# Attention, mixing and a channel network on one core: conversions spread later, other planner durations, 24 passes

## The chip, the cores and the metric

The kernel runs on one core of a Trainium2 chip. The time is what the device takes for one execution, in microseconds (us); a kernel's time is the median of its runs. TensorE does the matmuls and is called PE in the profile, with its weight loads apart (PEld); VectorE is DVE, ScalarE is ACT, GpSimd is POOL, and SyncE (SP) issues the transfers between DRAM and the core's memory.

## The reference

Three stages, one behind the other, in float32. The attention has windows: half of the heads see the last 32 positions, the others every fourth of the last 128.

```
B, H, S, D = 4, 8, 576, 64                 # q, k, v
a = softmax(mask(q @ k^T / 8)) @ v          # windowed; heads put side by side: x is (4, 576, 512)
xk = mu_k*x + (1-mu_k)*x_prev;  xr = mu_r*x + (1-mu_r)*x_prev      # x_prev: one position earlier
x = sigmoid(xr @ w_r) * (relu(xk @ w_k)**2 @ w_v)                   # 512 -> 1024 -> 512
u = x + (x^T @ U @ V)^T                                             # U 576x32, V 32x576
out = u + relu(u @ w_ch1) @ w_ch2                                   # 512 -> 2048 -> 512
```

## The kernel before

**Phase one** is the attention and the mixing step. The mixing step works on eight chunks of 288 positions. Chunk 0 multiplies whole float32 weights (L811). From chunk 1 on each operand is split into a high and a low part, and a product is three matmuls, L814 (high by high), L815 (low weight), L816 (low input). The splits of the twenty weight pieces are `hi_lo` by way of `sub`, and the subtraction is L348 on VectorE (`wl<-wx,wh`). A chunk is 20 steps, called quanta: four `r` tiles (they need weight pieces 1 to 4), eight `k` tiles (pieces 5 to 12), and the `v` tiles (13 to 20), 24 matmuls for two such steps of eight products. Inside each chunk two *visits* bring the attention forward, two units at a time out of 32: scores `qk` (L675, `psS<-raw`), masks and row maxima on VectorE (L536), exponentials on ACT, the inverse of the row sums on VectorE (L550, L551), normalisation on POOL (L556), transposes on PE (`tr`, L713), a copy of them on ACT (`pts`), and the product with v (`pv`, L731). So the matmuls of attention come in packs of up to 160 small ones between the large ones of the mixing step.

**The weights** come as 64-bit words and are converted on the chip by `cv_bits`: one operation on ACT (L384) and four on VectorE (L385, L386, L388, L391). `jobs` is the list of these: 20 for the mixing weights, then 32 for the channel network (`cv_w2`, whose result goes back to DRAM as `w2f`, L418), one for U and two for V. `convert_to(n)` brings the list forward to job n; in chunk c from 1 on it is called in every quantum with 20 + 0.35 times the number of quanta since chunk 1 began.

**Phase two** starts while phase one ends: y is read back, the U step and the V step follow (L907, L925, L926, L943; L948 adds to `us`), u goes through DRAM (`uf`) and comes back as `ug`. The channel network multiplies in combined blocks: the sums of weight blocks (L471) feed `ch1` (L1035 to L1037), split rows (`rh`, `rl`, L348) feed `ch2` (L1112 to L1114).

**The order of the work** isn't that of the code. Each operation is only recorded, with its engine, a duration that the code estimates, what it reads and writes, and sometimes `lock=True` (VectorE and POOL are planned not to run two such operations at once). `plan()` then goes through the list forwards, taking what can start first by those durations, computes backwards how late each could be, and repeats with that as the rank, `PASSES` times in all; the order with the earliest planned end is written out, for every engine. Where the plan sees PE wait for more than 900 ns ahead of an operation that opens a bank, it puts filler matmuls by a tile of zeros there (L1304), for half of that time. Their number so depends on the planned durations, and nothing else that is issued on PE changes in number with the plan.

Of the kernel before, what the change touches and what calls it, by code (L numbers as in the profile page):

```python
# [18 lines left out]
NCH = 2 * B  # L19
# [37 lines left out]
VISIT0 = (4, 12)  # L57
VISIT = (1, 10)
CONV0 = [min(20, 7 + n) for n in range(20)]
W2RATE = 0.35  # L60
SIDE_AT = 9
SPLIT = (-4, -4, -3, -3, -1, -1, 0, 0, 1, 1, 2, 2, 5, 5, 6, 6, 7, 7, 8, 8)
SPLIT_ENG = ("DVE",)
# [6 lines left out]
LATE = 1500.0  # L70
FILL, FILL_FROM, FILL_NS = 0.5, 900.0, 0.453
PLAN_PRINT = None
PASSES = 10
RATE = 285.0


# [1 line left out]
def tile_attention_mix_channel(  # L78
# [44 lines left out]
    def op(eng, ns, fn, r=(), w=(), more=100, lock=False, mode=None, size=0):  # L123

        o = Op()
        o.eng, o.ns, o.fn, o.r, o.w, o.more, o.lock, o.mode, o.size = eng, ns, fn, list(r), list(w), more, lock, mode, size
        ops.append(o)
# [214 lines left out]
    def sub(eng, n, out_, a, b, r, w, psum=False, fr=True):  # L342

        if eng == "POOL":
            t = 50 + 2.45 * n if fr else 110 + 1.93 * n
            op("POOL", t, lambda: nc.gpsimd.tensor_tensor(out=out_(), in0=a(), in1=b(), op=ALU.subtract), r, w, 40, lock=True)  # L346
        else:
            dve(n, lambda: nc.vector.tensor_tensor(out=out_(), in0=a(), in1=b(), op=ALU.subtract), r, w, two=True, psum=psum)  # L348
# [228 lines left out]
    def attend(u):  # L577

        b, part, pair = unit(u)
        nw, kc, starts, mk = unit_kind(pair, part)
        raw = raws.pop(u)
        sc = [bank("S") for _ in range(2)]
        pr = Lazy([P, 10 * KW], F32, "pr", "pr", 4)
        mn, sm = Lazy([P, 5], F32, "mn", "mn", 3), Lazy([P, 5], F32, "sm", "sm", 3)
        pt, ov = bank("S"), bank("S")
        pts = Lazy([P, 5 * P], F32, "pt", "pts", 2)

        def qk():  # L590
            for w in range(nw):
                for e in range(2):
                    r = head(e)
                    k0 = nw * QW + starts[w]
                    slot, h = (w // 4, w % 4) if w < 8 else (2, 2 * e + w - 8)
                    nc.tensor.matmul(
                        sc[e]()[h * QW : (h + 1) * QW, slot * KW : (slot + 1) * KW],
                        lhsT=raw()[r, w * QW : (w + 1) * QW], rhs=raw()[r, k0 : k0 + KW], start=True, stop=True,
                    )

        pe(nw * 2 * 40, qk, [(raw, 0)], [(x,) for x in sc], "qk")
        yield
        slots = [(e, s_ * KW, (2 * s_ + e) * KW, mk[s_]) for s_ in range(2) for e in range(2)]

        def lows():
            for i, (e, c, d, m) in enumerate(slots):
                low(sc[e](), c, pr(), d, m, mn(), i)
            for e in range(2):
                low(sc[e](), 2 * KW, pr(), 4 * KW, mk[2], mn(), 4, head(e))

        def exps():
            for i in range(5):
                exp(pr(), i * KW, mn(), sm(), i)

        def norms():
            norm(pr(), 4 * KW, sm(), 4, 1, 5 * KW)
            norm(pr(), 0, sm(), 0, 5)

        op("DVE", 6 * LOW, lows, [(x,) for x in sc] + [("cst",)], [(pr,), (mn,)], 170)
        op("ACT", 5 * EXP, exps, [(pr,), (mn,)], [(pr,), (sm,)], 190, mode="exp")  # L620
        op("DVE", 260, lambda: inv(sm(), 5), [(sm,)], [(sm,)], 80)
        op("POOL", 360 + 6 * NORM, norms, [(pr,), (sm,)], [(pr,)], 40, lock=True)
        yield

        def tr():
            for i in range(3):
                nc.tensor.transpose(pt()[:, i * P : (i + 1) * P], pr()[:, i * P : (i + 1) * P], ident)

        pe(3 * 108, tr, [(pr,), ("cst",)], [(pt,)], "tr")
        yield  # L630
        copy(3 * P, lambda: pts()[:, : 3 * P], lambda: pt()[:, : 3 * P], [(pt,)], [(pts, 0)], psum=True)
        yield

        def pv():
            for w in range(nw):
                for e in range(2):
                    r = head(e)
                    c = (w // 4 * 4 + w % 4 if w < 8 else 8 + 2 * e + w - 8) * QW
                    nc.tensor.matmul(
                        ov()[r, w * QW : (w + 1) * QW], lhsT=raw()[r, QKW + w * D : QKW + (w + 1) * D],  # L640
                        rhs=pts()[r, c : c + QW], start=True, stop=True,
                    )

        pe(nw * 2 * 60, pv, [(pts, 0), (raw, "v")], [(ov,)], "pv")
        yield
        x_out(ov, pair, part, b)
        yield

    def attend2(ua, ub):
# [10 lines left out]
        sm = [Lazy([P, 5], F32, "sm", "sm", 3) for _ in range(2)]  # L660
        pt, ov = bank("S"), [bank("S") for _ in range(2)]
        pts = Lazy([P, 5 * P], F32, "pt", "pts", 2)
        ns = nw // 2
# [19 lines left out]
        for e in range(2):  # L683
            first_, own = (ns - 4, 0) if e else (0, 4)
            base = e * ns * KW

            def lows(e=e, first_=first_, own=own, base=base):
                for i in range(4):
                    low(sc[e](), i * KW, pr(), base + (first_ + i) * KW, mk[i // 2], mn[e](), first_ + i)
                if nw == 10:  # L690
                    for f in range(2):
                        low(sc[f](), (4 + e) * KW, pr(), base + own * KW, mk[2], mn[e](), own, head(f))

            def exps(e=e, base=base):
                for i in range(ns):
                    exp(pr(), base + i * KW, mn[e](), sm[e](), i)

            kp, ks = [(pr, e)], [(sm[e],)]
            op("DVE", (4 + 2 * (ns - 4)) * LOW, lows, [(x,) for x in (sc if nw == 10 else sc[e : e + 1])] + [("cst",)], kp + [(mn[e],)], 170)
            op("ACT", ns * EXP, exps, kp + [(mn[e],)], kp + ks, 190, mode="exp")  # L700
            op("DVE", 260, lambda e=e: inv(sm[e](), ns), ks, ks, 80)
            op("POOL", 180 + ns * NORM, lambda e=e, base=base: norm(pr(), base, sm[e](), 0, ns), kp + ks, kp, 40, lock=True)
        yield

# [435 lines left out]
    NQ = 20  # L1140
# [6 lines left out]
    NW = len(places)  # L1147
    jobs = []
    for i, j in places:
        jobs.append((w1raw[i][:, j * CW : (j + 1) * CW], CW, lambda raw, i=i, j=j: cv_weight(raw, (i, j))))  # L1150
    jobs += [
        (w2raw[i][:, j * CW : (j + 1) * CW], CW, lambda raw, i=i, j=j: cv_w2(raw, i, j)) for i in range(16) for j in range(2)
    ]
    jobs.append((upk, NT * RANK, cv_u))
    jobs += [(vpk[:, j * HS : (j + 1) * HS], HS, lambda raw, j=j: cv_v(raw, j)) for j in range(2)]
    loaded = []
    converted = 0
    AHEAD = 3
# [69 lines left out]
    for c in range(NCH - 1):  # L1228
        cur = quanta(c) if c else first
        for n in range(NQ):  # L1230
# [13 lines left out]
            for when, p, which in MIX:  # L1244
                if when == n + 1:
                    mix(c + 1, p, which)
    convert_to(len(jobs))


    prep = {}  # L1250
    for j in range(3):
# [2 lines left out]
        prep[at_ + 1] = lambda j=j: load_rows(2 * j, "DVE")  # L1254
        prep[at_ + 2] = lambda j=j: load_rows(2 * j + 1, "DVE")
    for i, fn in enumerate(quanta(NCH - 1)):
        fn()
        if side:
            side.pop(0)()
        if i in prep:  # L1260
            prep[i]()
    for fn in side:
        fn()

# [134 lines left out]
```

## Time and profile before

| | |
|---|---|
| median of 3 runs | 766.39 us (764.46 to 767.51) |
| the profiled execution | 765.77 us, span 763.9 us, mean granted clock 0.995 |
| PE busy | 739.0 us, 97% of the span, 6925 matmuls |
| VectorE busy | 570.7 us, 75%, 1335 instructions |
| ACT, POOL busy | 391.4 us (51%), 388.3 us (51%) |
| DMA | 109.77 MB, mean 144 GB/s |

The profile is one execution. Busy time is by engine; "idle before" is how long an engine did nothing ahead of a row, and the name behind the arrow is what ended that by the semaphores. "issue" there means that the profile has nothing to name. The granted clock is PE's, as a part of full speed. In the timeline, neighbouring rows of one kind are merged, with their number behind x.

### The profile page before, as it was taken

How to read it: one execution, taken by the hardware profiler on the slowest of the kernel's cores; microseconds unless marked ns; L12 is line 12 of the kernel's file. 1: busy time of each engine (PE TensorE's matmuls, PEld its weight loads, DVE VectorE, ACT ScalarE, POOL GpSimd, SP SyncE). 2: the span in 40 equal slices, each digit the busy share in tenths (PEclk: the TensorE clock that was granted, in tenths of full speed). 3: DMA queues.
4: the chain of work that ended last, by engine and by line, in shares of the span. 5: the costliest groups of instructions: out<-in, count | busy, mean ns of one | idle time of the engine just before them, and what ended most of it. 6: DMA issues, size and time to landing. Idle time of an engine off the chain costs nothing. (4 is left out here: it accounts for less than half of the span.)

```text
span 763.9 us, 18346 instructions
## 1 busy us (share of the span) xinstructions
PE 739.0 (97%) x6925; PEld 678.4 (89%) x6925; DVE 570.7 (75%) x1335; ACT 391.4 (51%) x995; POOL 388.3 (51%) x408
## 2 busy tenths in 40 slices
PE   7898999999999999999899999999999999999997
PEld 5776899899988999999899888888988999898986
DVE  6998999999998644465767789766888865575632
ACT  5686885757684755273444543443452433343310
POOL 1343345646463735274755677534677654456500
PEclk9999999999999999999999999999999999999999
DMA  9874648686867320355553244132432212042001
GB/s 334 275 259 164 204 156 282 210 270 210 281 209 218 117 87 2 124 174 187 178 162 123 71 157 146 56 110 88 162 103 98 84 56 84 28 139 65 19 1 55
DMA packets 53224, 109.77 MB, mean 144 GB/s; under 512 B 5649, under 2 KB 15889, under 8 KB 53137
## 3 DMA queue, kind: packets, MB, share of 16 engines
q1 hardware_dynamic: 53136, 108.62, 43.1%
q8 instruction: 54, 0.88, 0.5%
q14 instruction: 34, 0.27, 0.1%
HBM read 86.05 MB, written 22.54 MB: 142 GB/s over the span
## 5 line engine op out<-in xcount | busy, mean ns | idle before, releaser
L346 POOL TENSOR_TENSOR cl<-sums,ch 128x512 fp32r<-128x512 f32 x72 | 98.2, 1364 | 86.8 <-ACT ch L351 58.5
L1113 PE MATMUL psS<-hh,rl 128*128 128x512 f32 (+1 forms) x320 | 119.6, 374 | 2.6 <-DVE rl L348 2.6
L1114 PE MATMUL psS<-hl,rh 128*128 128x512 f32 (+1 forms) x320 | 119.8, 374 | 0.3 <-DVE hl L1050 0.2
L1112 PE MATMUL psS<-hh,rh 128*128 128x512 f32 (+1 forms) x320 | 119.6, 374 | 0.2 <-ACT hh L1091 0.2
L351 ACT ACTIVATE ch<-sums 128x512 fp32r<-128x512 f32 (+1 forms) x104 | 57.3, 561 | 105.6 <-DVE sums L471 99.9
L814 PE MATMUL psM<-xk,wh 128*128 128x288 f32 x336 | 100.7, 300 | 0.9 <-DVE y L876 0.9
L816 PE MATMUL psM<-xk,wh 128*128 128x288 f32 x336 | 98.9, 294 | 1.5 <-issue 1.5
L815 PE MATMUL psM<-xk,wl 128*128 128x288 f32 x336 | 99.1, 295 | 1.1 <-issue 1.1
L346 POOL TENSOR_TENSOR cl<-st,ch 128x256 fp32r<-128x256 f32 x80 | 66.6, 849 | 56.0 <-PE psM L1037 35.7
L471 DVE TENSOR_TENSOR sums<-st 128x256 f32<-128x256 f32 (+1 forms) x144 | 86.6, 650 | 9.2 <-POOL cl L346 5.6
L346 POOL TENSOR_TENSOR xk<-m,xk 128x288 fp32r<-128x288 f32 x56 | 53.0, 959 | 55.5 <-ACT xk L351 33.3
L1113 PEld LDWEIGHTS psS<-hh,rl 128*128 128x128 f32 x320 | 60.7, 190 | 12.2 <-DVE rl L348 2.8
L1114 PEld LDWEIGHTS psS<-hl,rh 128*128 128x128 f32 x320 | 60.7, 190 | 12.2 <-DVE hl L1092 1.0
L1112 PEld LDWEIGHTS psS<-hh,rh 128*128 128x128 f32 x320 | 60.6, 189 | 10.2 <-ACT hh L1091 0.6
L814 PE MATMUL psM<-k2s,wh 128*128 128x288 f32 x224 | 68.1, 304 | 0.3 <-DVE k L861 0.2
L815 PE MATMUL psM<-k2s,wl 128*128 128x288 f32 x224 | 66.8, 298 | 0.7 <-issue 0.7
L816 PE MATMUL psM<-k2s,wh 128*128 128x288 f32 x224 | 66.7, 298 | 0.0
L814 PEld LDWEIGHTS psM<-xk,wh 128*128 128x128 f32 x336 | 63.0, 187 | 3.1 <-issue 1.6
L816 PEld LDWEIGHTS psM<-xk,wh 128*128 128x128 f32 x336 | 63.2, 188 | 1.2 <-issue 1.2
L815 PEld LDWEIGHTS psM<-xk,wl 128*128 128x128 f32 x336 | 63.1, 188 | 0.1
L1072 DVE TENSOR_TENSOR ok<-ok,psM 128x256 f32<-128x256 f32 (+1 forms) x96 | 46.4, 504 | 20.8 <-PE psM L1037 18.6
L346 POOL TENSOR_TENSOR k2s<-k,k2s 128x288 fp32r<-128x288 f32 x49 | 45.2, 926 | 31.7 <-ACT k2s L351 29.4
(152 smaller groups left out, 2124.0 us busy)
## 6 DMA issues: line engine op xcount, KB each, us to landing
st<-w2f SPq DMA_DIRECT2D x96, 256.0 KB, 3.0
w<-w2raw SPq DMA_DIRECT2D x32, 512.0 KB, 4.8
w<-w1raw SPq DMA_DIRECT2D x20, 512.0 KB, 5.6
w2f<-w SPq DMA_DIRECT2D x32, 256.0 KB, 2.7
raw<-qk SPq DMA_DIRECT2D x16, 320.0 KB, 6.4
ytmp<-y SPq DMA_DIRECT2D x32, 144.0 KB, 3.1
yb<-ytmp SPq DMA_DIRECT2D x4, 1152.0 KB, 6.2
uf<-us SPq DMA_DIRECT2D x32, 144.0 KB, 1.9
```

Source lines behind the costliest of these rows:

```text
L346: op("POOL", t, lambda: nc.gpsimd.tensor_tensor(out=out_(), in0=a(), in1=b(), op=ALU.subtract), r, w, 40, lock=True)
L351: act(n, lambda: nc.scalar.activation(out_(), in_(), AF.Copy), r, w, psum, strided)
L471: dve(k * Q, lambda: nc.vector.tensor_tensor(out=q(sm_, n, k)(), in0=a(), in1=b(), op=op_), [(s1,), (s2,)], [(sm_, key)], two=True)
L814: nc.tensor.matmul(a, lhsT=wh, rhs=xh, start=start, stop=False)
L815: nc.tensor.matmul(a, lhsT=wl, rhs=xh, start=False, stop=False)
L816: nc.tensor.matmul(a, lhsT=wh, rhs=xl, start=False, stop=stop)
L1072: dve(k * Q, lambda: nc.vector.tensor_tensor(out=out_(), in0=a(), in1=b(), op=op_), r, w, two=True, psum=True)
L1112: nc.tensor.matmul(a, lhsT=wh, rhs=xh, start=(j == 0 and e == 0), stop=False)
L1113: nc.tensor.matmul(a, lhsT=wl, rhs=xh, start=False, stop=False)
L1114: nc.tensor.matmul(a, lhsT=wh, rhs=xl, start=False, stop=(j == 7 and e == 1))
```

## The change

The rate of the conversions is 0.28 a quantum for 0.35, and `convert_to` goes on through the last chunk; the jobs for U and V stand behind the first 25 of the 32 jobs of phase two. The planner takes 165 + 2.14 n ns for a subtraction of n columns on POOL, counts the inverse of the sums as `lock`, and runs 24 passes.

```diff
-W2RATE = 0.35
+W2RATE = 0.28
+UV_AT = 25
...
-PASSES = 10
+PASSES = 24
...
         if eng == "POOL":
-            t = 50 + 2.45 * n if fr else 110 + 1.93 * n
+            t = 165 + 2.14 * n if fr else 110 + 1.93 * n
...
-        op("DVE", 260, lambda: inv(sm(), 5), [(sm,)], [(sm,)], 80)
+        op("DVE", 260, lambda: inv(sm(), 5), [(sm,)], [(sm,)], 80, lock=True)
...
-            op("DVE", 260, lambda e=e: inv(sm[e](), ns), ks, ks, 80)
+            op("DVE", 260, lambda e=e: inv(sm[e](), ns), ks, ks, 80, lock=True)
...
-    jobs += [
+    w2_jobs = [
         (w2raw[i][:, j * CW : (j + 1) * CW], CW, lambda raw, i=i, j=j: cv_w2(raw, i, j)) for i in range(16) for j in range(2)
     ]
+    jobs += w2_jobs[:UV_AT]
     jobs.append((upk, NT * RANK, cv_u))
     jobs += [(vpk[:, j * HS : (j + 1) * HS], HS, lambda raw, j=j: cv_v(raw, j)) for j in range(2)]
+    jobs += w2_jobs[UV_AT:]
...
-    convert_to(len(jobs))
...
     for i, fn in enumerate(quanta(NCH - 1)):
+        convert_to(NW + int(((NCH - 2) * NQ + i + 1) * W2RATE))
         fn()
         if side:
             side.pop(0)()
         if i in prep:
             prep[i]()
+    convert_to(len(jobs))
```

The lines of the changed kernel are numbered one higher than before, down to the list of jobs. Three places show what the plan makes of it.

PE at the end of chunk 0 and the start of chunk 1, before (L811 is chunk 0's product, L1304 the filler, L814 and L815 the first of chunk 1):

```order
L675 MATMUL psS<-raw 32x64 x40
L811 MATMUL psM<-xk_293,wx 128x288 x16
L1304 MATMUL psM<-zero 128x512 x4
L811 MATMUL psM<-k_774,wx 128x288 x16
L713 MATMUL psS<-cst_t,pr 128x128 x5
L1304 MATMUL psS<-zero 128x512 x2
L731 MATMUL psS<-pts,raw 64x32 x40
L675 MATMUL psS<-raw 32x64 x40
L1304 MATMUL psM<-zero 128x224 x4
L811 MATMUL psM<-k_774,wx 128x288 x16
L713 MATMUL psS<-cst_t,pr 128x128 x5
L814 MATMUL psM<-xk,wh 128x288
L815 MATMUL psM<-xk,wl 128x288
```

The same place in the changed kernel (L812, L815, L816 are the same products there):

```order
L676 MATMUL psS<-raw 32x64 x40
L812 MATMUL psM<-xk_293,wx 128x288 x4
L812 MATMUL psM<-k_762,wx 128x288 x24
L714 MATMUL psS<-cst_t,pr 128x128 x5
L812 MATMUL psM<-k_762,wx 128x288 x4
L732 MATMUL psS<-pts,raw 64x32 x40
L676 MATMUL psS<-raw 32x64 x40
L812 MATMUL psM<-k_762,wx 128x288 x4
L815 MATMUL psM<-xk,wh 128x288
L816 MATMUL psM<-xk,wl 128x288
L817 MATMUL psM<-xk,wh 128x288
L815 MATMUL psM<-xk,wh 128x288
```

The fillers are gone here, the last piece of attention before chunk 1 comes four products earlier, and one pack of transposes no longer stands ahead of chunk 1.

VectorE at that time, before, from the end of a row of masks (L536) to the weight splits (L348, `wl<-wx,wh`):

```order
L536 ISA pr,mn<-psS,cst_t 64x64
L536 ISA mn 64x1
L348 TENSOR_TENSOR wl<-wx,wh 128x512
L876 TENSOR_TENSOR y<-psM,sg 128x288
L768 SCALAR_TENSOR_TENSOR m<-d,mu_t,x_95 128x288
L550 TENSOR_SCALAR sm<-sm 128x5
L551 RECIPROCAL sm<-sm 128x5
L348 TENSOR_TENSOR wl<-wx,wh 128x512
L876 TENSOR_TENSOR y<-psM,sg 128x288
L768 SCALAR_TENSOR_TENSOR m<-d,mu_t,x_964 128x288
L550 TENSOR_SCALAR sm<-sm 128x5
L551 RECIPROCAL sm<-sm 128x5
L348 TENSOR_TENSOR wl<-wx,wh 128x512 x3
```

And in the changed kernel (L349 is the split, L537 the mask):

```order
L769 SCALAR_TENSOR_TENSOR m<-d,mu_t,x_95 128x288
L877 TENSOR_TENSOR y<-psM,sg 128x288
L769 SCALAR_TENSOR_TENSOR m<-d,mu_t,x_95 128x288
L349 TENSOR_TENSOR wl<-wx,wh 128x512
L877 TENSOR_TENSOR y<-psM,sg 128x288
L769 SCALAR_TENSOR_TENSOR m<-d,mu_t,x_95 128x288
L349 TENSOR_TENSOR wl<-wx,wh 128x512 x3
L769 SCALAR_TENSOR_TENSOR m<-d,mu_t,x_95 128x288
L349 TENSOR_TENSOR wl<-wx,wh 128x512
L877 TENSOR_TENSOR y<-psM,sg 128x288
L537 ISA pr,mn<-psS,cst_t 128x64
L537 ISA mn 128x1
```

The masks that stood ahead of the first split now stand behind the fifth, and the two inverse pairs are not among the splits.

VectorE in the last chunk, where phase two begins, before (L471 the first sums, L948 the additions of the U and V step):

```order
L768 SCALAR_TENSOR_TENSOR m<-d,mu_t,x_3263 128x288
L348 TENSOR_TENSOR k2s<-k_1488,k2s 128x288
L768 SCALAR_TENSOR_TENSOR m<-d,mu_t,x_3263 128x288
L348 TENSOR_TENSOR yl<-psS,yh 64x512
L768 SCALAR_TENSOR_TENSOR m<-d,mu_t,x_3263 128x288
L471 TENSOR_TENSOR sums<-st 128x256
L768 SCALAR_TENSOR_TENSOR m<-d,mu_t,x_3263 128x288
L471 TENSOR_TENSOR sums<-st 128x256
L348 TENSOR_TENSOR g<-psS,g 32x512
L876 TENSOR_TENSOR y<-psM,sg 128x288 x2
L948 TENSOR_TENSOR us<-psS,yb 128x288 x2
L876 TENSOR_TENSOR y<-psM,sg 128x288
L948 TENSOR_TENSOR us<-psS,yb 128x288
```

And in the changed kernel, from the like place on (L386, L387, L389 and L392 are a conversion's four operations, L472 the sums, L949 the additions):

```order
L349 TENSOR_TENSOR k2s<-k_1351,k2s 128x288
L769 SCALAR_TENSOR_TENSOR m<-d,mu_t,x_3210 128x288
L349 TENSOR_TENSOR g<-psS,g 32x512
L386 TENSOR_SCALAR w_4805<-w_4805 128x512
L877 TENSOR_TENSOR y<-psM,sg 128x288
L387 TENSOR_SCALAR w_4805<-w_4805 128x512
L472 TENSOR_TENSOR sums<-st 128x256
L389 SCALAR_TENSOR_TENSOR w_4805<-w_4172,w_4805 128x512
L949 TENSOR_TENSOR us<-psS,yb 128x288 x2
L877 TENSOR_TENSOR y<-psM,sg 128x288
L392 SCALAR_TENSOR_TENSOR w_4805<-w_4172,w_4805 128x512
L386 TENSOR_SCALAR w_4828<-w_4828 128x512
```

Between the same sums and additions there are now conversions.

## Rows read from the trace of the kernel before

**Rows 1.** The page, section 1: busy us, share of the span, instructions, by engine

```profile
PE 739.0 (97%) x6925; PEld 678.4 (89%) x6925; DVE 570.7 (75%) x1335; ACT 391.4 (51%) x995; POOL 388.3 (51%) x408
```

**Rows 2.** Busy time by stretch: stretch, length, engines (instructions), granted clock, DMA share, GB/s

```profile
50.00:100.00 50.00, 46.52 (x601) 39.24 (x579) 47.35 (x151) 37.91 (x115) 16.83 (x20) 1.00 0.61 204
...
250.00:300.00 50.00, 50.00 (x674) 48.98 (x673) 25.85 (x86) 30.69 (x90) 25.52 (x35) 1.00 0.21 71
...
300.00:350.00 50.00, 50.00 (x370) 48.90 (x369) 29.07 (x56) 27.35 (x58) 27.04 (x31) 1.00 0.39 126
```

**Rows 3.** Timeline, PE: start, us, line, operation, [idle before <- releaser]

```profile
89.48 0.40 PE L814 MATMUL psM<-xk,wh 128*128 128x288 f32 x1 [0.93 <-DVE y L876]
...
177.21 0.29 PE L815 MATMUL psM<-xk,wl 128*128 128x288 f32 x1 [1.05 <-issue]
...
196.95 0.40 PE L815 MATMUL psM<-k2s,wl 128*128 128x288 f32 x1 [0.72 <-issue]
...
215.58 0.29 PE L816 MATMUL psM<-xk,wh 128*128 128x288 f32 x1 [1.54 <-issue]
215.71 0.29 PE L814 MATMUL psM<-xk,wh 128*128 128x288 f32 x1
...
232.83 0.30 PE L675 MATMUL psS<-raw 64*32 64x64 f32 x4 [1.80 <-issue]
```

**Rows 4.** Busy time between the five waits of rows 3

```profile
89.48:177.21 87.73, 85.77 (x1148) 83.76 (x1149) 84.69 (x234) 58.66 (x172) 46.29 (x52) 1.00 0.69 221
177.21:196.95 19.74, 19.02 (x255) 18.48 (x254) 19.63 (x64) 15.19 (x42) 13.26 (x15) 1.00 0.77 253
196.95:215.58 18.63, 17.09 (x254) 16.69 (x255) 17.47 (x56) 12.45 (x42) 8.20 (x11) 1.00 0.81 264
215.58:232.83 17.25, 15.45 (x256) 15.08 (x256) 16.25 (x29) 13.61 (x37) 11.34 (x13) 1.00 0.67 211
```

**Rows 5.** The page, section 3: the instruction queue's packets, MB, share of 16 DMA engines

```profile
q8 instruction: 54, 0.88, 0.5%
```

**Rows 6.** Timeline, PE: a piece of attention ahead of the wait at 177.21

```profile
173.67 1.37 PE L731 MATMUL psS<-pts,raw 64*64 64x32 f32 x80
174.97 0.86 PE L675 MATMUL psS<-raw 64*32 64x64 f32 x64
175.75 0.40 PE L814 MATMUL psM<-xk,wh 128*128 128x288 f32 x1
```

**Rows 7.** Busy time by stretch: behind the last wait, and a later visit

```profile
232.80:236.00 3.20, 3.17 (x17) 3.08 (x17) 2.08 (x24) 2.79 (x10) 1.15 (x2) 0.61 0.88 231
262.00:272.00 10.00, 10.00 (x191) 9.70 (x190) 5.40 (x24) 8.03 (x18) 7.02 (x11) 1.00 0.04 13
```

**Rows 8.** Timeline, PE: waits before the first products of chunk 1

```profile
69.61 0.55 PE L713 MATMUL psS<-cst_t,pr 128*128 128x128 f32 x3 [1.59 <-POOL pr L556]
...
82.73 0.55 PE L713 MATMUL psS<-cst_t,pr 128*128 128x128 f32 x3 [0.52 <-POOL pr L556]
83.03 0.38 PE L814 MATMUL psM<-xk,wh 128*128 128x288 f32 x1
```

**Rows 9.** Timeline, DVE: two groups of weight splits

```profile
81.44 3.00 DVE L348 TENSOR_TENSOR wl<-wx,wh 128x512 fp32r<-128x512 f32 x3
...
85.97 1.28 DVE L348 TENSOR_TENSOR wl<-wx,wh 128x512 fp32r<-128x512 f32 x2
```

**Rows 10.** Busy time of line 536 alone, 12 masks and 12 reads

```profile
75.60:77.82 2.22, 2.08 (x24) 1.00 0.99 328
```

**Rows 11.** Busy time of the tile w alone (conversions of phase two)

```profile
73.00:235.00 162.00, 80.62 (x118) 20.83 (x31) 0.00 (x0) 1.00 0.71 229
```

**Rows 12.** Timeline, PE: a wait for data inside chunk 2

```profile
147.76 0.55 PE L713 MATMUL psS<-cst_t,pr 128*128 128x128 f32 x3 [0.56 <-POOL pr L556]
```

**Rows 13.** Timeline, DVE and PE: the phase boundary

```profile
367.90 1.30 DVE L1017 TENSOR_TENSOR tmp<-ug 128x512 f32<-128x512 f32 x2 [4.11 <-DMA ug<-uf]
...
379.54 0.39 PE L1113 MATMUL psS<-hh,rl 128*128 128x256 f32 x1 [2.61 <-DVE rl L348]
```

## The prediction

> **What bounds the kernel now.** I read the page's first section before anything else. TensorE's matmuls are busy for 739.0 of the span's 763.9 us [rows 1], so a gain must come out of the 24.9 us in which they are not, or out of matmuls at the lower clock, or out of filler matmuls. Next the busy time by stretch: between 50 and 100 us PE is busy for 46.52 of 50 and VectorE for 47.35; from 250 to 350 PE doesn't idle at all and VectorE is down to 25.85 and 29.07 [rows 2]. The work that the change takes later goes there.
>
> Then I listed PE's waits in order of time. Five of them stand out: 0.93, 1.05, 0.72, 1.54 and 1.80 us, at 89.48, 177.21, 196.95, 215.58 and 232.83 us [rows 3]. Four have no releaser that the profile knows ("issue"); the 0.93 is put down to VectorE. Count the matmuls between them: 1148, 255, 254, 256 [rows 4], that is 9, 2, 2 and 2 times some 128. A wait for data would not keep to such a grid. The page has 54 packets of 0.88 MB on the instruction queue [rows 5], 16 KB each; 6925 matmuls and as many weight loads [rows 1] are 13,850 instructions, and over 54 that is 256 apiece, or 128 matmuls. So I read these waits as PE waiting for its next block of instructions.
>
> Why at these and not at the other 45 edges? Each stands just behind a piece of attention, whose matmuls pass in 16 ns each (80 in 1.30 us, 64 in 0.78 us by their starts), where the mixing products before and after take 0.13 us each [rows 3, 6]. A block of 128 that is nearly all attention is used up in 2.0 us, one of products in 17. By my count along PE's order the blocks before the five waits hold 127, 127, 113, 114 and 128 attention matmuls: 2.0, 2.0, 3.7, 3.6 and 2.0 us long. With the wait behind each, a block took 2.9, 3.1, 4.4, 5.1 and 3.8 us to come, in stretches with a DMA share of 0.67 to 0.81 [rows 4]. A block of the same make at 262 to 272 us, share 0.04 [rows 7], has no wait. So: a wait where a whole visit of attention falls into one block while the DMA engines are busy.
>
> **The change, part by part.** The sum is made against the profiled execution, 765.77 us; it lies 0.6 under the median of 766.39.
>
> *Fillers, and with them the grid.* The planner, with 24 passes and other durations, now finds less room in front of chunk 0's matmuls and writes 22 fewer filler matmuls, all before the first of the five waits, and it shifts what stands around each visit. The ends of the visits against the block edges were 1, 15, 14, 4 and 3 matmuls off the nearest edge; by the same count they are now 23, 49, 36, 30 and 19 off for most of the busy stretch. The blocks there hold 105, 79, 92 and 98 attention matmuls: the rest, 23 to 49 products at 0.13 us, makes them 4.6 to 7.6 us long, against the 2.9 to 5.1 us that a block took to come. Those waits go: before, the five cost 6.0 us together. One later block, near 245 us, keeps 127 attention matmuls, a wait of 0 to 1.8; with the DMA still busy there I take 1.2. Another early block of 3.4 us may wait; I take 0.3.
> The clock goes with it. Behind the 1.80 us wait the granted clock reads 0.61 over 3.2 us [rows 7], so most of that stretch ran at the lower of the two levels, 1.2 GHz for 2.4. The 17 matmuls in it, the last 4 of the attention and 13 products, would take 4 x 0.016 + 13 x 0.133 = 1.8 us at the upper one: 1.4 lost. For a wait of 1.2 us I take 0.5, since only the longest of the five shows such a row. So 7.4 us before, 2.0 after: -5.4. Bounds: -7.4 (none is left) to +1.0 (they only move, and one more appears).
> The Trainium skill speaks against this term: "Runtime: NRT & Kernel Launch", Instruction fetch mechanics, says that the sequencer fetches 16 KiB blocks of 256 instructions ahead of use and that the cost of crossing a boundary is "mostly hidden". By that rule this term would be near 0 and the sum near -1.1. The block size agrees with the 54 packets and the counts of 254 to 256; for "hidden" the waits of 0.72 to 1.80 us at those edges decide, as far as the releaser "issue" can be read so.
>
> *VectorE's order at the first chunk's end.* The first mixing products of chunk 1 need the first four weight splits. In before the fourth stands inside the group at 81.44 us, and products start at 83.03 behind waits of 1.59 and 0.52 us for POOL's normalisation [rows 8, 9]. In the new order 12 mask operations with their 12 reads, two inverse pairs and two L768 no longer stand ahead of the fourth split: such a group of 12 masks and 12 reads holds VectorE for 2.08 us [rows 10]; the rest, at 0.3 a pair and 0.4 an L768 by their starts, for 1.4: 3.5 us. But ahead of the eighth split the counts come out level (the masks are in again), and the k products, which need it, may not start before about 87.3 us, the end of the split group of 85.97 [rows 9]. In before they start some 3.2 us after 89.48, at 92.7; the new order has one piece of attention (2.8 us) less in front of them. So PE can get there at most 92.7 - 2.8 - 87.3 = 2.6 us better, 0.9 of it the wait at 89.48 that is already counted. I take -1.7; bounds -4 (ahead of the sixteenth split VectorE has 26 operations fewer, and all of it may show) to +1 (the lost fillers leave PE waiting in their place).
>
> *Conversions at 0.28 a quantum.* Nothing is added: 32 jobs as before. One job is 80.62 us over 118/4 on VectorE, 2.73 us [rows 11]. Before, jobs end with quantum 100 of 140; now with 125. Seven jobs, 19 us, leave the stretch where VectorE is full and land where it has 20 us of room in each 50 [rows 2]. What it gives PE before 235 us: only the waits for data there, 0.56 us at 147.76 [rows 12] and a few tenths. The replanned chunks may as well have one such piece more as one less; a piece in one of six chunks cost 0.9, I take +0.6, bounds -1 to +1.5.
> U and V go before the last seven w2 jobs, so the U step doesn't wait for the later ones. `lock` for the inverses keeps them out of POOL's way in the plan only; POOL's new cost and 24 passes add no instruction. 0, beyond the order counted above.
>
> *Phase boundary.* u and ug go through DRAM; VectorE waits 4.11 us for ug and PE 2.61 us for VectorE's split behind it [rows 13]. The order there is nearly as before: 0, bounds -1 to +2 here, the dearer case is a rival.
>
> Sum: -5.4 - 1.7 + 0.6 = -6.5, so 759.3 for the execution and, 0.6 above it, 759.9 for the median.
>
> **The rivals.**
> A, the grid is an accident or the blocks wait elsewhere: only the start and the data waits count, 766.4 - 1.1 = 765.3. For it: "issue" names no cause, and 0.93 us has a data releaser; edges move with every matmul, so others can be hit. Against it: four counts in a row on multiples of 128. The rule of the Trainium skill that is quoted above ("Runtime: NRT & Kernel Launch") would end here too.
> B, VectorE holds the start as before (47.35 of 50 busy [rows 2], and level counts at the eighth split): 766.4 - 5.4 + 0.6 = 761.6.
> C, slower: the last conversions delay the phase boundary. In the new order five jobs stand among the first sums (L471) and the additions that make u (L948); the stores of u, ug's load and the w2f reads that the sums need queue on SP behind their loads. If nothing hides them, u comes 5 x 2.73 = 13.7 us later, and PE with it: 759.9 + 13.7 = 773.6. For it: VectorE's wait for ug is already 4.11 us, so the chain is late today. Against it: VectorE idles 24 and 21 us in the two stretches from 250 to 350 [rows 2]. It decides from a delay of about 11 us on, where the gain above is gone and half a per cent more.
> D, the planner's order is no better on the chip than before: 766.4.
>
> **How the numbers follow.** Forecast 0.45; B 0.14; A 0.17; D 0.08; C 0.11; 0.05 for a larger gain (all waits gone, start -4: 754). Half a per cent, 3.8 us, is about what a measurement of this kernel tells from no change: faster is under 762.6, slower above 770.2. Faster: 0.42 of the forecast's 0.45 + 0.09 of B's 0.14 + the 0.05 + 0.03 from A's lower end = 0.59. Slower: C's share above 770.2 with 0.02 from the others: 0.12. Same: 0.29. The range is 754 to 768: below, the larger gain; above, A and D with the upper bounds of the small terms, C left out. The likeliest case alone: 757 to 762.
>
> **What would show it.** Right: at the counts of the old grid, no "issue" waits above 0.5 us between 170 and 240 us, and PE idle 6 us lower; the granted clock 1.00 from 100 to 240 us; the first L814 earlier than 83.0 us, k products from about 87 to 90; VectorE's w tile work reaching to about 340 us. Wrong: "issue" waits of the same sum on another multiple of 128 (A); PE busy at its end but started at 83 (B); a wait for ug over 8 us or PE waiting at 356 to 380 us for sums, rh or us (C).

## The result, and the profile after

The changed kernel takes 757.91 us (median of 6 runs, 757.27 to 761.51) against 767.32 for the kernel before in the same comparison: ratio 0.9896, 95% interval 0.9869 to 0.9922, about 8.0 us by the ratio and 9.4 by the medians. Forecast were 759.9 and a gain of 6.5. The profiled execution has a span of 756.0 us for 763.9. Three executions of 1437 to 1446 us, one each of the kernel before, b_spread and a_noclamp below, do not count in the ratios.

Three stages can be compared by PE's timeline: from the start to the first product of chunk 1, from there to the last product of the mixing step, and the rest.

| | before | after | difference | forecast |
|---|---|---|---|---|
| first product of chunk 1 at | 83.0 | 83.4 | +0.4 | -1.7 |
| from it to the last product | 272.8 | 265.9 | -6.9 | -4.8 |
| from it to the span's end | 408.1 | 406.6 | -1.5 | 0 |

So most of the gain sits in the stretch where the five waits were. Busy time by stretch, the kernel after (columns as in [rows 2]; 350 us is where its mixing step has ended):

```profile
0.00:83.00 83.00, 73.05 (x1036) 55.26 (x1037) 71.27 (x234) 55.51 (x171) 24.12 (x36) 0.96 0.75 257
83.00:350.00 267.00, 265.07 (x3295) 259.79 (x3294) 222.95 (x619) 175.52 (x498) 144.71 (x167) 1.00 0.55 184
100.00:250.00 150.00, 150.00 (x2277) 147.47 (x2271) 140.94 (x424) 106.71 (x324) 85.45 (x99) 1.00 0.64 212
```

The like stretches of the kernel before:

```profile
0.00:83.00 83.00, 72.80 (x1064) 56.15 (x1065) 71.71 (x256) 57.55 (x190) 26.88 (x40) 1.00 0.76 263
83.00:356.00 273.00, 266.06 (x3286) 260.16 (x3285) 217.99 (x594) 173.07 (x480) 140.87 (x163) 0.99 0.55 178
100.00:250.00 150.00, 143.98 (x1955) 140.57 (x1954) 142.25 (x398) 101.09 (x292) 81.27 (x91) 0.99 0.71 229
```

PE idled 6.94 us between chunk 1's start and the end of the mixing step, now 1.93; between 100 and 250 us it idled 6.02, now not at all. Just ahead of that window the kernel after has a wait for data, the longest left in its mixing step:

```profile
99.80 1.37 PE L732 MATMUL psS<-pts,raw 64*64 64x32 f32 x80 [1.05 <-ACT pts L352]
```

The waits of PE, longest first, in the kernel after, answer to [rows 3, 8] (us in total, times, longest): no row names "issue" any more.

```profile
PE psM L828 <- DVE xk L769: 3.0, 2, 2.5
PE psM L812 <- ACT sg L352: 1.6, 1, 1.6
PE psS L640 <- ACT pts L352: 1.6, 2, 1.4
PE psS L1308 <- DVE zero L1304: 1.5, 1, 1.5
PE psS L1113 <- DVE us L949: 1.1, 1, 1.1
PE psS L732 <- ACT pts L352: 1.1, 1, 1.1
```

At the phase boundary, timeline of VectorE and PE, kernel after (answering to [rows 13]): VectorE's wait for ug is longer, PE's is shorter.

```profile
361.65 1.30 DVE L1018 TENSOR_TENSOR tmp<-ug 128x512 f32<-128x512 f32 x2 [4.66 <-DMA ug<-uf]
363.34 1.30 DVE L349 TENSOR_TENSOR rl<-st,rh 128x512 fp32r<-128x512 f32 x1
...
363.37 0.38 PE L1113 MATMUL psS<-hh,rh 128*128 128x256 f32 x1 [1.11 <-DVE us L949]
```

The split `rl` comes right behind ug at 363.34; in the kernel before PE stood 2.61 us for one [rows 13]. And the fillers are fewer, as counted: 6903 matmuls for 6925.

### The profile page after: what moved, and what is told of

The parts are those of the page before. It is cut to its first block, busy times and chain, and to the rows that moved or that the text cites. A ratio compares the mean times of both kernels' runs of the same rounds, so it can differ in the third digit from the quotient of the medians.

```text
span 756.0 us, 18304 instructions
## 1 busy us (share of the span) xinstructions
PE 736.8 (97%) x6903; PEld 675.2 (89%) x6903; DVE 569.9 (75%) x1335; ACT 392.3 (52%) x995; POOL 386.9 (51%) x408
## 5 line engine op out<-in xcount | busy, mean ns | idle before, releaser
L815 PE MATMUL psM<-xk,wh 128*128 128x288 f32 x336 | 101.0, 301 | 0.0
L816 PE MATMUL psM<-xk,wl 128*128 128x288 f32 x336 | 99.1, 295 | 0.0
L472 DVE TENSOR_TENSOR sums<-st 128x256 f32<-128x256 f32 (+1 forms) x144 | 85.9, 644 | 8.0 <-POOL cl L347 3.9
L347 POOL TENSOR_TENSOR xk<-m,xk 128x288 fp32r<-128x288 f32 x56 | 54.6, 990 | 33.9 <-ACT xk L352 24.5
L815 PE MATMUL psM<-k2s,wh 128*128 128x288 f32 x224 | 67.3, 301 | 0.0
L816 PE MATMUL psM<-k2s,wl 128*128 128x288 f32 x224 | 66.0, 295 | 0.0
L817 PE MATMUL psM<-k2s,wh 128*128 128x288 f32 x224 | 65.9, 294 | 0.0
L815 PEld LDWEIGHTS psM<-xk,wh 128*128 128x128 f32 x336 | 63.0, 187 | 0.6
L816 PEld LDWEIGHTS psM<-xk,wl 128*128 128x128 f32 x336 | 63.1, 188 | 0.1
L1093 DVE SCALAR_TENSOR_TENSOR hl<-ort,hh 128x512 fp32r<-128x512 f32 x32 | 26.2, 819 | 48.3 <-ACT hh L1092 48.3
```

The costliest lines, as they stand in the source:

```text
L472: dve(k * Q, lambda: nc.vector.tensor_tensor(out=q(sm_, n, k)(), in0=a(), in1=b(), op=op_), [(s1,), (s2,)], [(sm_, key)], two=True)
L815: nc.tensor.matmul(a, lhsT=wh, rhs=xh, start=start, stop=False)
L816: nc.tensor.matmul(a, lhsT=wl, rhs=xh, start=False, stop=False)
L817: nc.tensor.matmul(a, lhsT=wh, rhs=xl, start=False, stop=stop)
```

## The experiments

Theory G: a block of instructions that is nearly all attention is used up before the next one has come, so a shift of the blocks by some matmuls decides. Its first rival, F: data and transfers made those waits. For the start, theory V: VectorE's work sets when chunk 1 begins; its rival, P: PE's own chain or the weights' arrival. In the labels, b_ stands for the kernel before and a_ for the changed one. Times of the kernel before lie at 766.6 to 767.9 in the three series. Stages are read from one profiled execution of each kernel. A pad (a filler matmul put in to shift the rest) costs time at the start, so the shifted kernels are compared from the first product of chunk 1 to the last of the mixing step ("the mixing stretch", 272.8 before, 265.9 after).

**The kernel before, shifted by 100 and by 128 matmuls.**

```diff
             onto, wide, many = getattr(o, "before", (None, 0, 0))
+            groups += many > 0
+            for _ in range(PAD if many and groups == 2 else 0):
+                nc.tensor.matmul(onto()[:32, :64], lhsT=zero[:64, :32], rhs=zero[:64, :64], start=True, stop=True)
```

PAD = 100 (b_pad100):

> The kernel before with 100 tiny filler matmuls (32 columns of weights, 64 columns wide, some 16 ns each) ahead of its second piece of scores, near 8 us, where PE waits for data anyway; the order of all else is kept. Theory G (the five waits are block edges of PE's instructions that fall on the end of a visit of attention): the ends of those five visits move from 0, 127, 112, 113 and 4 matmuls behind an edge to 100, 100, 85, 85 and 104, so no block of the busy stretch is nearly all attention; the waits of 0.93, 1.05, 0.72, 1.54 and 1.80 us and the low clock behind the last are gone: 7.4 us, less up to 1.5 for the pads: 759.5 to 762 us. Theory F (it is transfers and data: later conversions and the new order took the waits away): nothing changes but the pads, 766.5 to 768.5 us, waits at the same places.

PAD = 128 (b_pad128):

> The same with 128 tiny matmuls, one whole block by theory G, so every later matmul has its old place in its block. G: the five waits stand where they stood, behind the same visits, 5 to 6 us together: 766.5 to 768.5 us. F: the same time. It is the control for b_pad100: by G the two differ by 5 to 8 us though 28 tiny matmuls more stand in this one.

Measured: 767.87 us, ratio 0.9996 (0.9968 to 1.0025), and 771.97, 1.0053 (1.0020 to 1.0086). In neither did the total come as expected: the pads took 55 ns each (100 in 5.54 us) and 34 ns (128 in 4.39 us), not 16, and chunk 1 began at 90.5 and 87.6 us instead of 83.0. The waits named "issue" did as G says. PE's timeline with 100 pads, every row with an "issue" wait in the whole mixing step, and three waits for data that are new or longer:

```profile
81.39 0.43 PE L676 MATMUL psS<-raw 64*32 64x64 f32 x16 [1.46 <-issue]
...
215.70 1.14 PE L732 MATMUL psS<-pts,raw 64*64 64x32 f32 x64 [0.80 <-ACT pts L352]
...
228.22 0.40 PE L815 MATMUL psM<-k2s,wh 128*128 128x288 f32 x1 [0.56 <-DVE k L862]
...
257.94 1.37 PE L732 MATMUL psS<-pts,raw 64*64 64x32 f32 x80 [1.91 <-ACT pts L352]
```

With 128 pads, the rows with an "issue" wait:

```profile
182.28 0.29 PE L816 MATMUL psM<-xk,wl 128*128 128x288 f32 x1 [1.25 <-issue]
...
201.60 0.40 PE L816 MATMUL psM<-k2s,wl 128*128 128x288 f32 x1 [0.31 <-issue]
...
219.75 0.29 PE L817 MATMUL psM<-xk,wh 128*128 128x288 f32 x1 [1.04 <-issue]
...
237.82 0.43 PE L676 MATMUL psS<-raw 64*32 64x64 f32 x4 [2.62 <-issue]
```

With a whole block of pads the four stand before the same matmuls as in [rows 3], 4 to 5 us later, and behind the last of them the granted clock is 0.51 over 3.2 us; with 100 they are gone, that clock is 1.00, and one wait has come at 81 us, at the visit that now fills a block. For these four that is direct evidence for the blocks. The traces of all kernels of this document bear it out: they hold 29 "issue" waits of more than 0.2 us, and the number of matmuls ahead of each of the 29, counted from the start, is 70 to 86 more than a multiple of 128.

The fifth wait, 0.93 us at 89.48, is another matter. With 128 pads it is there too (0.93), with 100 it is 0.18 us, but in the two kernels of the next experiment, whose edges lie elsewhere, the same matmul still waits for VectorE's y:

```profile
100.50 0.40 PE L814 MATMUL psM<-xk,wh 128*128 128x288 f32 x1 [0.57 <-DVE y L876]
...
91.40 0.40 PE L814 MATMUL psM<-xk,wh 128*128 128x288 f32 x1 [0.85 <-DVE y L876]
```

So it is in the main the wait for data that the profile names. The mixing stretch is 273.0 us with 128 pads, as before, and 268.9 with 100: 3.9 us gained, though the four waits, 5.1 us, and some 1.4 of low clock (the forecast's estimate) went. The rest came back as the waits for ACT and VectorE above; that this work had run ahead while PE stood, and was now late itself, is likely and not shown.

**The changed kernel, shifted by 40 and by 128** (a_pad40, a_pad128), with the same lines.

> The changed kernel with 40 tiny filler matmuls at the same place. G: the ends of five visits between 150 and 235 us come to 119, 17, 118, 4 and 10 matmuls behind an edge, so waits of 0.7 to 1.8 us with the releaser issue appear behind four or five of them: 762 to 766 us. F: 757.5 to 759 us, PE without idle time between 105 and 300 us as in the changed kernel.

> The changed kernel with 128 tiny matmuls, one whole block by theory G. G and F: no wait between 105 and 300 us, 757.5 to 759.5 us. It is the control for a_pad40: by G it is 4 to 7 us faster than that one though it issues 88 matmuls more.

Measured: 761.50 us, 0.9896 (0.9865 to 0.9927), and 761.76, 0.9916 (0.9888 to 0.9945). With 40 pads the first product of chunk 1 is at 83.8, and these three waits stand in the mixing stretch, which is 268.6 us long, 2.7 more than without pads; their sum is 2.95:

```profile
157.85 0.40 PE L818 MATMUL psM<-k2s,wh 128*128 128x288 f32 x1 [1.46 <-issue]
...
211.71 0.31 PE L677 MATMUL psS<-raw 64*32 64x64 f32 x6 [0.57 <-issue]
...
228.58 0.41 PE L677 MATMUL psS<-raw 64*32 64x64 f32 x12 [0.92 <-issue]
```

G named five places; three waited, the blocks of 2.1 and 3.1 us between them did not. With 128 pads there is no "issue" wait, as expected, but chunk 1 starts 2.8 us later and the mixing stretch is 1.5 us longer: its wait for `pts` is 1.39 us (1.05 without pads), and the granted clock behind it is 0.50 for 3.4 us. As a control by the total it missed: it is not 4 to 7 us faster than the kernel with 40 pads, whose 761.50 us lie between the ranges of G and F and whose ratio is that of the changed kernel. What speaks for G in this pair are the places of the waits.

**The kernel before with 99 more and with 25 fewer filler matmuls** (b_split99, b_cut25). In the first each filler of 512 columns is cut into four of 128; in the second the 22 narrow fillers at 29 us and three near 73 us go:

```diff
+            if wide < CW and many > 20:
+                many = 0
+            elif wide < CW and many == 4:
+                many = 1
             for _ in range(many):
```

> The kernel before with each of its 33 fillers of 512 columns cut into four of 128: 99 matmuls more for the same columns, so that the blocks move as in b_pad100 without its pads' time. G (waits at block edges): the waits at 89, 177, 197, 216 and 233 us and the low clock behind the last go, 7 us; the visit at 71 to 74 us now fills a block alone and waits some 1.5 us; cutting the fillers costs 0 to 2 us: 760.5 to 764 us. F (the waits come from data and traffic): 766 to 769 us.

> The kernel before without its 22 narrow fillers near 29 us and 3 of the 4 near 73 us: 25 matmuls fewer, about what the change takes out (22), in the old order with the old conversions. G: the blocks at visits between 85 and 250 us last 4.5 us or more, but the visit at 70 to 74 us now fills one (2.0 us): the five waits go, one of 0.5 to 1.5 us comes near 72 us; the start by itself no sooner (V): 759 to 763 us. F (the order and the traffic of the conversions made the gain): 765.5 to 768 us.

Measured: 776.22 us, 1.0144 (1.0080 to 1.0209), and 769.11, 1.0022 (0.9992 to 1.0052): both totals missed. Cut fillers take 0.22 us each for 128 columns (28 in 6.23 us at the start), and chunk 1 of the first kernel begins at 94.4. Without the 25, PE runs slowly near 33 us, timeline of PE and busy time of 6 us there (granted clock 0.50, the lower level, 1.2 GHz):

```profile
32.86 4.21 PE L827 MATMUL psM<-xk,wx 128*128 128x288 f32 x8 [4.33 <-DVE xk L768]
```

```profile
32.00:38.00 6.00, 5.14 (x13) 3.89 (x14) 5.46 (x13) 1.64 (x9) 1.44 (x2) 0.50 0.74 271
```

The eight products take 4.21 us behind an idle 4.33; elsewhere eight take 2.21. Its runs go from 762.3 to 775.4 with mean clocks of 0.994 to 0.981, and the profiled one is the 762.3. The mixing stretch is shorter in both, as G says: 269.6 and 269.7 us, 3.1 to 3.2 less than before. The four old "issue" places are free of waits; new ones are at 62.20 and 85.27 us in the first (0.52, 1.06) and at 76.21 us (1.17) in the second. The second has one more that G did not forecast, behind a block that should last 4.5 us or more:

```profile
234.87 0.29 PE L814 MATMUL psM<-k2s,wh 128*128 128x288 f32 x1 [0.54 <-issue]
```

So dropping some 22 fillers, as the change does, would not have been a gain by itself: the grid they shift is worth 3 to 4 us of the mixing stretch, and what they did for the clock is lost.

**The two parts of the change apart** (b_planner, b_spread). First the planner's part alone (24 passes, POOL's duration, `lock`), then the later conversions alone, each on the kernel before; the diffs are the lines shown under "The change".

> The planner's part of the change alone: POOL's subtraction, lock at the inverses, 24 passes; conversions at 0.35 as before. Counted along its order, its blocks at visits between 115 and 250 us last 3.8, 5.0, 2.0, 3.7, 4.4, 2.9, 2.0 and 3.1 us. G: three to five waits of 0.5 to 1.8 us behind those of 2.0 to 3.1, 3 to 5 us together, so most of the gain isn't there: 763 to 767 us. If the planner's better durations were the cause as such: 758 to 760 us.

> The other part alone: conversions at 0.28 through the last chunk, U and V behind 25 of 32, the planner's durations and 10 passes as before. Counted along its order the blocks at visits last 3.2, 4.4, 2.3, 4.3, 5.6 and 2.4 us (the last near 245 us). G: one or two waits of 0.5 to 1.5 us: 760 to 764 us. If spreading as such were the cause: 757.5 to 759.5 us; if it is nothing without the planner: 766 to 768 us.

Measured: 767.81 us, 1.0019 (0.9993 to 1.0046), and 765.65, 0.9982 (0.9958 to 1.0007). Neither part gains anything by itself. The planner's part has four "issue" waits and a long wait for data:

```profile
129.50 0.40 PE L814 MATMUL psM<-xk,wh 128*128 128x288 f32 x1 [2.42 <-DVE y L876]
...
168.99 0.65 PE L675 MATMUL psS<-raw 64*32 64x64 f32 x16 [3.51 <-issue]
...
205.21 0.40 PE L815 MATMUL psM<-k2s,wl 128*128 128x288 f32 x1 [0.56 <-issue]
...
223.33 0.29 PE L816 MATMUL psM<-xk,wh 128*128 128x288 f32 x1 [1.02 <-issue]
...
240.82 0.42 PE L675 MATMUL psS<-raw 64*32 64x64 f32 x13 [0.98 <-issue]
```

Ahead of the 2.42 us at 129.50 the count is 64 more than a multiple of 128, some 16 short of the edge, so VectorE's y is the cause there. The four others are 6.1 us of "issue" waits, 5.1 before. Three stand behind blocks that the count made 2.0 to 2.9 us long; the 0.56 stands behind one of 4.4, and one of 3.1 had none. Its mixing stretch is 277.4 us, and the stretch behind it 403.7, 4.4 shorter than before. The spread part has three small "issue" waits, 0.67, 0.35 and 0.72, where the count put blocks of 3.2, 2.3 and 2.4 us, and loses elsewhere. Its timeline, PE, then VectorE there, then PE at the phase boundary:

```profile
271.05 1.79 PE L1308 MATMUL psS<-zero 128*128 128x512 f32 x7
272.68 0.38 PE L714 MATMUL psS<-cst_t,pr 128*128 128x128 f32 x2
274.95 0.44 PE L714 MATMUL psS<-cst_t,pr 128*128 128x128 f32 x2 [1.89 <-POOL pr L557]
```

```profile
272.50 0.46 DVE L877 TENSOR_TENSOR y<-psM,sg 128x288 f32<-128x288 f32 x1 [0.93 <-DMA ytmp<-y]
272.87 0.68 DVE L389 SCALAR_TENSOR_TENSOR w<-w,w 128x512 int32<-128x512 int32 x1
273.47 0.16 DVE L551 TENSOR_SCALAR sm<-sm 128x4 f32<-128x4 f32 x1
```

```profile
378.00 0.58 PE L1114 MATMUL psS<-hh,rl 128*128 128x256 f32 x1 [2.81 <-DVE rl L349]
```

A late conversion (L389) and a product's output that waits for its transfer stand ahead of the inverse that POOL and then PE wait for; fillers (1.8 us) and waits (1.89, and 0.37 behind it) cost PE some 4 us there. This is rival C's kind of collision, in chunk 6 and not at the phase boundary. In the changed kernel the same conversions are as late, and no such wait is there: its order puts them elsewhere.

**The changed kernel with 10 passes, and with the old durations** (a_passes10, a_olddur).

> The changed kernel with 10 passes of the planner. Counted along its order its blocks at visits between 110 and 235 us last 2.8, 3.1, 2.9, 2.0, 5.8, 2.3, 2.0 and 2.0 us. G: four to six waits named issue, 4 to 8 us together: 762 to 767 us. If the durations and the spreading carry the gain by themselves: 757.5 to 760 us.

> The changed kernel with the old durations (POOL's subtraction, no lock at the inverses), 24 passes and the spread conversions. Its blocks at visits last 2.6, 2.5, 2.0 and 2.0 us between 110 and 165 us, 5.8 or more from there to 235. G: two to four waits between 110 and 165 us, 2 to 5 us, and, if the wait for rl at the phase boundary of b_spread belongs to the old durations, that one too: 761 to 767 us. If 24 passes and the spreading carry the gain: 757.5 to 760 us.

Measured: 758.81 us, 0.9910 (0.9883 to 0.9938), and 769.61, 1.0038 (1.0017 to 1.0059). G missed the first: seven short blocks were counted, and only two waits came, 0.24 and, at 196.75, 1.88 us. So a short block makes a wait possible and does not forecast it. In the total the 14 passes more are worth nothing that these runs can tell. But the two kernels come to it by different ways: with 10 passes chunk 1 starts at 80.97 us, 2.5 sooner, the mixing stretch is 271.2 us, 5.2 longer, and the rest 404.6, 2.0 shorter. With the old durations the total is 11 us higher than in the kernel after, 9.7 of it in the mixing stretch (275.6 us): the timeline has three "issue" waits, of which the last was not forecast, and the stall of b_spread again:

```profile
127.74 0.24 PE L676 MATMUL psS<-raw 64*32 64x64 f32 x1 [0.81 <-issue]
...
147.29 0.30 PE L676 MATMUL psS<-raw 64*32 64x64 f32 x3 [2.29 <-issue]
...
249.86 0.41 PE L676 MATMUL psS<-raw 64*32 64x64 f32 x10 [1.16 <-issue]
...
279.18 0.44 PE L714 MATMUL psS<-cst_t,pr 128*128 128x128 f32 x2 [1.69 <-POOL pr L557]
```

**Less work for VectorE** (a_noclamp, a_nc_all). The clamp in `cv_bits` (L385) is left out, first in the changed kernel's own order, then with a new plan. The first was meant for the mixing weights only, but `cv_bits` sets `xt_` in its first line, so the condition of this edit always holds: VectorE issues 1280 instructions for 1335, and all 55 clamps are gone in both kernels.

```diff
-        dve(n, lambda: nc.vector.tensor_scalar(x(), x(), HI_MIN, HI_MAX, op0=ALU.max, op1=ALU.min), kx, kx)
+        dve(n, (lambda: None) if xt_ is not None else
+            lambda: nc.vector.tensor_scalar(x(), x(), HI_MIN, HI_MAX, op0=ALU.max, op1=ALU.min), kx, kx)
```

> The changed kernel in its own order, but the clamp of the 20 conversions of the mixing weights (L386 on wx) is not issued: 20 x 0.535 us = 10.7 us less on VectorE before 80 us, no other change (the weights here need no clamp). Theory V (VectorE holds the start, so its new order gave nothing by 100 us): chunk 1 starts 3 to 8 us earlier, 750 to 755 us. Rival P (PE's own chain of scores, normalisation and copies, or the arrival of the weights, holds it): chunk 1 starts less than 1 us earlier, 757 to 758.5 us.

> The changed kernel planned and run without the clamp in any conversion (no weight here needs it; values below 2^-127 or above 2^128 would no longer be clamped): 55 operations, some 29 us less on VectorE, 10.7 of them before 80 us. Its blocks at visits last 4.5 us or more but one near 240 us. V and G: the start gains as in a_noclamp, no issue wait above 0.7 us but perhaps near 240 us: 747 to 753 us. If the plan matters more than VectorE's load: anything from 753 to 760 us.

Measured: 751.95 us, 0.9796 (0.9752 to 0.9839), and 750.78, 0.9780 (0.9745 to 0.9815). Both kernels start chunk 1 sooner, as V says and P does not. In the first it is 6.4 us earlier than in the kernel after, and VectorE has 63.1 us of work ahead of it for 71.7; PE's timeline:

```profile
77.07 0.51 PE L816 MATMUL psM<-xk,wh 128*128 128x288 f32 x1
```

Not all of the 6.4 need be VectorE's, for the granted clock was 1.00 up to there, and 0.96 in the kernel after. There eight products of chunk 0, behind an idle 2.48 us, took 3.86 us; here they take 2.21. Timeline of PE in the kernel after:

```profile
16.71 3.86 PE L828 MATMUL psM<-xk,wx 128*128 128x288 f32 x8 [2.48 <-DVE xk L769]
```

And the amount of work is not the only thing that counts. Busy time (columns as in [rows 2]) up to the first product of chunk 1, in a_noclamp, a_nc_all and b_spread:

```profile
0.00:77.07 77.07, 69.75 (x1038) 53.14 (x1039) 63.10 (x219) 55.68 (x174) 24.55 (x37) 1.00 0.81 277
0.00:80.96 80.96, 72.58 (x1036) 55.10 (x1036) 64.01 (x211) 55.65 (x172) 23.82 (x36) 0.96 0.78 265
0.00:80.69 80.69, 71.81 (x1060) 55.94 (x1061) 71.40 (x254) 54.54 (x172) 26.77 (x38) 1.00 0.78 270
```

The first two have nearly the same work for VectorE and start 3.9 us apart, with another order and another clock. b_spread has the work and the clock of the kernel before and starts 2.3 us sooner than it, in another order.

The mixing stretch is 264.5 and 264.3 us, 1.4 to 1.6 less than in the kernel after, and the two times can't be told apart. Both beat the kernels of the comparison, for weights that need no clamp.

## Why the prediction was right, point by point

The total was forecast well, 1.4 us short of the profiled gain of 7.9, but this is in part luck: the start came out 2.1 us worse than forecast, the mixing stretch 2.1 and the phase boundary 1.5 us better.

*The five waits and the clock, -5.4.* The mechanism is shown for the four "issue" waits: shifted by 100, 99 or -25 the old kernel loses them, shifted by a whole block it keeps them, and the new kernel shifted by 40 gets three. The fifth, 0.93 us, the forecast took for a block edge; it was in the main a wait for y. The size was too low: the block near 245 us, for which 1.2 + 0.5 us were kept, did not wait (the DMA share from 245 to 250 us is 0.12; the forecast took the transfers to go on), nor did the early one. The four waits, 5.1 us, and by the forecast's estimate 1.4 of low clock went, and no new "issue" wait came: 6.5 of the 6.9 us. PE's waits for data in the mixing stretch are as large as before, 1.8 and 1.9 us; the last 0.4 has no row of its own. What the argument lacked is that the gain could only stand because no new waits for data came with it: in the old order 2.6 to 3.4 us of 6.5 came back as waits for ACT and VectorE.

Two conditions of the forecast are weaker than it has them. A busy DMA does not decide: in a_passes10 a block of 2.0 us that ends near 216.5 us was followed by no wait, with a share of 0.75 from 212 to 217 us, and in a_olddur 1.16 us were waited behind a block with a share of 0.03 (246.6 to 248.6 us; 0.71 during the wait). And the time that a block takes to come, 2.9 to 5.1 us there, assumes that its transfer starts when PE enters the block before, which no run shows.

Rival A falls, for the same runs. The Trainium skill ("Runtime: NRT & Kernel Launch", Instruction fetch mechanics) calls the cost of crossing a block "mostly hidden". That holds for most of the 54 blocks here; where a visit fills most of a block it often does not, by 0.2 to 3.5 us each.

*VectorE's order at the first chunk's end, -1.7.* This step failed; it gave +0.4. The -1.7 was priced at the k products. These begin at 90.06 us for 92.78, but one piece of attention now stands behind them and no longer ahead, and the wait of 0.93 is gone; of the 1.7 nothing is left. The step took the start of chunk 1 to follow the splits. The fourth split came at 80.32 us, some 2 us sooner than before, but PE was not there: chunk 0's long products, which ran from 39.44 us in the kernel before, now begin only at 46.50, timeline of PE after:

```profile
46.50 10.22 PE L812 MATMUL psM<-xk,wx 128*128 128x288 f32 x40 [1.63 <-ACT sg L352]
```

From there on PE runs without a gap to chunk 1. The waits of 1.59 and 0.52 us [rows 8] were traded for longer ones before 47 us and a clock of 0.96 to 83 us (1.00 before; how much of the start this took is not known): 73.05 us busy for 72.80. VectorE is busy for 71.27 us of these 83, before for 71.71. So it came out as rival B says, the start as before; its sign was VectorE's 47.35 of 50 us [rows 2]. That VectorE's work holds the start is shown in part: with 8.6 us less of it chunk 1 starts 6.4 us sooner in the same order, the clock's share included. But an order can move the start too: b_spread, with the work of the kernel before, starts at 80.69 us. So a gain of 1.7 was within reach, and this order did not bring it.

*Conversions at 0.28, +0.6.* Between 100 and 250 us PE's waits for data are gone, but the 1.05 us at 99.80 and 0.65 at 302.83 came: 1.9 us in the whole stretch for 1.8, so about 0. The runs on the parts show that it depends on the rest of the order: with the old durations the late conversions cost PE some 4 us in chunk 6. The planner's edits, costed at 0 "beyond the order counted above", decide 11 us of the total in combination (a_olddur); why the small changes of POOL's durations and `lock` lead the plan to a better order was not tried, nor which of the two does.

*Phase boundary, 0.* It gave -1.5: PE's wait of 2.61 and the clock of 0.61 over the 3.5 us behind it became a wait of 1.11 for `us`. The wait for `rl`, 2.1 to 2.9 us, is in every kernel with the old durations and 10 passes, b_spread among them, and in none with either the new durations (a_passes10, b_planner) or 24 passes (a_olddur). So it belongs to the planner's part. Rival C did not come: VectorE waits 4.66 us for ug, not over 8, and the last loads of raw weights are issued at 271.6 us. A wait for `us` between 356 and 380 us was named as a sign of C and is there, 1.11 us; it was a poor sign, since b_pad128, with the old conversions, waits 1.6 us for it.

Of the other signs, no "issue" wait, the clock of 1.00 and the k products came as named; the first product before 83.0 us did not, and VectorE begins its last work on the tile w at 315.4 us, not near 340.

## What to carry to other kernels

Where a profile shows waits without a releaser, count the instructions between them: if the counts are multiples of one number, the engine may be waiting for its instructions. Shifting the program by a part of that number and by the whole of it tells. What helps is to keep a run of very short instructions from filling one block, by shifting them by a few. In the old order here that gave 3 to 4 us of the mixing stretch, and adding or dropping fillers for it cost at least as much elsewhere.

Before pricing an engine's new order, sum its work up to the point in question. If it was busy nearly all the time, a new order has little room: here the start of chunk 1 lay between 80.7 and 83.5 us in three orders (b_spread, before, after) with 71.4 to 71.7 us of VectorE's work, and taking work away gave more.

A change to a planner's numbers is a new draw of the whole order: of five mixtures of the same edits here two gained 7 to 8 us, two nothing, and one lost 3, so each has to be run.

## What was not expected of the hardware

- Small filler matmuls are dear in PE's first 20 us. One of 64 columns with 32 columns of weights took 55 ns in b_pad100 (100 in 5.54 us) and 34 in b_pad128 (128 in 4.39), where the attention's matmuls take 16 later on; what makes the two differ is open. Seven fillers of 512 columns took 3.36 us in the kernel before and the next eight 2.11; cut into 28 and 32 of 128 columns, in b_split99, they took 6.23 and 7.09.
- PE's first 10 us are not free though it waits there: 5.5 us of pads delayed chunk 1 by 7.5 (b_pad100) and 4.4 us by 4.6 (b_pad128), while 2.0 us delayed it by 0.3 (a_pad40). That the first scores are the head of the chain that VectorE works through is the likely reason and not shown.
- Behind blocks of much the same make, some 2 us long, PE waited for the next between not at all (near 247 us in the kernel after, at a DMA share of 0.12, and near 216.5 us in a_passes10, at 0.75) and 3.51 us (b_planner). What sets this was not measured by itself.
